# A new order for the first batch's steps and transfers in an attention and dense kernel on one core

## The chip, the cores and the metric

The kernel runs on one core of a Trainium2 chip. The core has a matrix engine (PE, TensorE), three engines for the rest (DVE or VectorE, ACT or ScalarE, POOL or GpSimd) and an engine that issues transfers (SP). Each works through a queue of its own in the order in which the program was written. The metric is the device time of one execution in microseconds (us), the median of three runs.

## What is computed

```python
def _attn_ref(q, k, v):                      # each (8, 8, 576, 64)
    k_p = k.reshape(B, H, Sp, pool, D).mean(axis=3)     # pool = 8: 72 keys
    v_p = v.reshape(B, H, Sp, pool, D).mean(axis=3)
    scores = scale * np.matmul(q, k_p.transpose(0, 1, 3, 2))
    scores = scores - np.max(scores, axis=-1, keepdims=True)
    attn = np.exp(scores)
    attn = attn / (np.sum(attn, axis=-1, keepdims=True) + 1e-09)
    return np.matmul(attn, v_p)
...
    x = attn_out.transpose(0, 2, 1, 3).reshape(B * S, H * D)     # 4608 x 512
    h = x @ w_in                                                  # 512 x 2048
    g = h * (1.0 / (1.0 + np.exp(-1.702 * h)))
    return g @ w_out                                              # 2048 x 512
```

Each batch's attention gives 576 rows of `x`; the dense layer takes these rows in chunks of 512.

## The kernel before

The work is written as a list of small steps. A table, `ORDER` (from line 27), names all 4763 of them in one row: `V:nm0_0#2` is the third `nm` step of batch 0, piece 0, on DVE. The letters are A for ACT, V for DVE, G for POOL, P for PE, D for a transfer that SP issues and O for an output; a star gives the step to the other engine that can do it. `Plan.order` (line 555) takes the steps by name in this order, and each engine's queue is what is left of the list when only its own steps are read. A step that stands later on its engine never overtakes one that waits. A second table, `WARMS` (line 462), puts extra passes of PE in front of named steps (16 ahead of the first `tps`, of two passes each); they multiply a constant, `ident`, by itself into a tile that nobody reads then, `warm` (`keep_warm`, line 2115).

The first batch runs through these steps, whose names the text uses:

- `kv`, `tl`, `q`: transfers of keys and values, of the rows that are left over at the end of the 576, and of queries. `raw`: a part of the weights, 512 KB of 64-bit numbers, `raw0`, `raw1` and so on.
- `red`: sums over windows of eight keys. DVE does the first key tile (`red0_k0`, line 882), PE the others (line 892) by multiplying with `ident`. `kbd`, `vbd` (line 928), `tps` (PE, line 958) and `tbd` (line 967): the sums spread into blocks, and the same of the left-over rows.
- `kps`, `k` and `qps`, `qt`: transposes on PE, and their copies on ACT or DVE.
- `sps`: scores on PE (line 1136). `nm` (line 1159): the negative maximum; `sc` (1167): the subtraction; `exp` on ACT (1188); sums (1193), the inverse, and `main` and `tail` (1208), the weights of the softmax in two groups of keys, on DVE.
- `tpt`, `apt` (PE, 1280): transposes of these; `at`, `ah` (1310, 1358): their copies; `pav` (PE, 1383, 1386): the product with the values; `x` (1423 on ACT, 1426 on DVE): the operand of the dense layer in two parts.
- Decoding of a part of the weights: ACT `e` and `raw` (1611, 1618), DVE `e` and `raw` (1624, 1630), POOL `raw` (1637), a cast `w` (1644, ACT or DVE) and POOL's `w` (1651). 32 parts go through it in all.
- `h` (PE, 1685 to 1687): the first product of the dense layer, in three passes, and `o` (1727 to 1729): the second.

Of PE's accumulators a pool `ps_o` of four banks holds, under one name `o`, the tiles `tps`, `qps`, `sps`, `tpt` and `apt` of this batch, the warm passes' tile and the dense layer's `o` tiles. A second pool of two banks holds `red`, the decoder's `e` and `h`; a third one of two `kps` and `pav`. A tile takes a bank when the one before it in that bank has been read. The warm passes' tile is made when the first pass is emitted, which `WARMS` puts ahead of `tps`, and it later serves as the accumulator of one row block of `o`.

```python
    warm = buf(ps_o, [P, DM], F32, "o", "warm")

    def keep_warm():
        nc.tensor.matmul(warm()[:, 0:P], lhsT=ident, rhs=ident, start=True, stop=True)
```

Of the kernel before, what the change touches and what calls it, by code (L numbers as in the profile page):

```python
# [27 lines left out]
D:raw#0 V:members#0 D:kv0#1 D:kv0#0 D:kv0#3 V:red0_k0#0 P:warm#0 D:tl0#0 D:tl0#1 A:e#0 V:at0_1#0 V:kbd0#0 D:kv0#2  # L28
V:e#0 P:tps0#0 D:q0_0#1 D:raw#1 P:red0_k1#0 V:tbd0#0 V:at0_0#0 A:raw#0 D:q0_0#0 D:raw#2 V:raw#0 P:kps0_0#0 D:kv0#5
P:qps0_0#0 V:kbd0#1 A:e#1 P:qps0_0#1 A:raw#1 G:raw#0 V:e#1 *A:qt0_0#0 A:k0_0#0 P:kps0_1#0 V:raw#1 D:raw#4 P:sps0_0#0  # L30
A:qt0_0#1 P:sps0_0#1 V:nm0_0#0 A:w#0 A:k0_1#0 P:qps0_0#2 V:nm0_0#1 G:w#0 V:sc0_0#0 D:kv0#4 A:e#2 A:qt0_0#2 P:qps0_0#3
P:sps0_0#2 V:e#2 D:kv0#6 D:kv0#7 D:q0_2#0 A:raw#2 A:qt0_0#3 V:sc0_0#1 V:raw#2 D:q0_1#1 P:sps0_0#3 A:e#4 D:q0_1#0
D:raw#6 A:raw#4 D:raw#5 V:nm0_0#2 D:raw#3 G:raw#1 V:e#4 V:nm0_0#3 P:red0_v0#0 A:sc0_0#0 V:sc0_0#2 V:raw#4 G:raw#2
P:red0_v1#0 D:raw#8 V:sc0_0#3 P:qps0_1#1 P:qps0_1#0 V:vbd0#0 D:raw#7 A:sc0_0#1 V:sps0_0#0 A:w#1 A:w#2 V:sps0_0#1
D:raw#13 A:qt0_1#1 G:raw#4 V:sps0_0#2 A:qt0_1#0 V:main0_0#3 V:main0_0#2 D:raw#10 V:tail0_0#0 A:e#6 V:main0_0#1
V:main0_0#0 P:tpt0_0#0 A:at0_0#0 V:vbd0#1 G:w#2 *A:w#4 V:e#6 D:qr1_0#3 D:qr1_0#6 P:apt0_0#2 P:sps0_1#0 A:ah0_0#2
P:apt0_0#3 V:nm0_1#0 D:qr1_0#1 A:at0_1#0 *A:ah0_0#3 A:raw#6 D:raw#12 P:pav0_0#2 V:raw#6 A:e#5 V:e#5 G:w#4 P:pav0_0#3
P:apt0_0#0 D:qr1_0#2 A:raw#5 D:tl1#1 A:x0_0#2 P:qps0_1#2 V:sc0_1#0 D:raw#9 A:e#3 D:qr1_0#4 P:apt0_0#1 V:x0_0#2
D:raw#11 A:ah0_0#0 A:x0_0#3 V:raw#5 A:raw#3 V:e#3 P:pav0_0#0 A:ah0_0#1 G:raw#6 P:sps0_1#1 V:x0_0#3 D:raw#14 A:e#8
G:w#1 D:raw#20 P:pav0_0#1 P:qps0_1#3 A:qt0_1#2 D:qr1_0#0 A:x0_0#0 P:sps0_1#2 A:raw#8 V:raw#3 G:raw#5 V:e#8 A:e#7  # L40
A:x0_0#1 V:x0_0#0 A:raw#7 D:raw#17 V:raw#8 V:e#7 D:raw#16 V:x0_0#1 V:raw#7 G:raw#3 P:h0_0#0 V:nm0_1#1 D:raw#15
P:h0_0#1 P:h0_0#2 A:w#6 P:h0_0#3 D:raw#18 P:h0_0#4 A:w#3 P:h0_0#5 A:e#10 V:nm0_1#2 G:raw#8 V:sc0_1#1 V:e#10 A:qt0_1#3
A:raw#10 G:w#6 P:h0_0#6 G:w#3 P:h0_0#7 V:raw#10 V:sc0_1#2 P:sps0_1#3 A:w#8 P:h0_0#8 P:h0_0#9 A:sc0_1#0 P:h0_0#10
A:g0_0#0 D:raw#22 P:h0_0#11 V:nm0_1#3 V:sc0_1#3 D:qr1_0#7 P:h0_0#12 V:sps0_1#0 P:h0_0#13 *A:gh0_0#0 G:raw#7 G:w#8
G:raw#10 *G:gl0_0#0 D:raw#21 A:sc0_1#1 *A:w#10 P:h0_0#14 D:qr1_0#5 *A:w#5 D:kv1_0#1 G:w#10 P:h0_0#15 D:raws#2
V:sps0_1#1 P:h0_0#16 A:g0_0#1 V:sps0_1#2 V:main0_1#1 P:h0_0#17 A:gh0_0#1 G:w#5 P:h0_0#18 A:e#9 D:tl1#0 D:raws#1
A:raw#9 P:h0_0#19 V:tail0_1#0 A:w#7 P:o0_0#0 P:o0_0#1 V:main0_1#0 P:h0_0#20 V:main0_1#2 D:raw#19 P:h0_0#21 P:h0_0#22
P:tpt0_1#0 P:apt0_1#0 G:gl0_0#1 P:o0_128#0 P:o0_128#1 D:kv1_0#0 V:e#9 A:ah0_1#0 A:at0_1#1 V:raw#9 *A:at0_0#1 A:e#11
D:raw#26 P:apt0_1#1 A:ah0_1#1 G:w#7 A:raw#11 P:h0_0#23 A:g0_0#2 V:main0_1#3 P:pav0_1#0 V:e#11 A:x0_1#0 V:raw#11 A:e#12
P:o0_0#2 *A:left0_1#0 *A:gh0_0#2 G:raw#9 V:x0_1#0 A:w#9 V:e#12 G:gl0_0#2 P:pav0_1#1 P:o0_128#2 A:raw#12 P:apt0_1#2  # L50
P:o0_0#3 A:e#14 G:w#9 *A:x0_1#1 A:ah0_1#2 D:raw#23 P:o0_128#3 V:raw#12 V:x0_1#1 V:e#14 D:raw#25 P:apt0_1#3 A:e#13
A:raw#14 V:e#13 P:o0_0#4 V:raw#14 A:left0_1#1 A:ah0_1#3 G:raw#12 V:qt1_0#0 A:raw#13 V:raw#13 P:pav0_1#2 A:e#15
A:raw#15 P:pav0_1#3 P:h0_256#0 A:x0_1#2 A:x0_1#3 G:raw#11 V:e#15 V:raw#15 A:e#16 V:x0_1#2 D:qr1_0#11 G:raw#13
P:h0_256#1 A:raw#16 V:x0_1#3 G:raw#14 P:o0_128#4 P:h0_256#2 A:left0_1#2 P:h0_256#3 P:h0_256#4 V:e#16 P:h0_256#5 A:w#11
V:raw#16 *A:w#12 V:qt1_0#1 P:h0_256#6 P:tps1#0 P:h0_256#8 P:h0_256#7 G:raw#16 D:qr1_0#14 *G:w#11 A:g0_256#0 P:h0_256#9
P:h0_256#10 A:gh0_256#0 P:h0_256#11 V:tbd1#0 A:e#21 P:o0_128#5 V:red1_0#0 P:h0_256#12 D:kv1_1#1 V:e#21 A:w#13 V:kbd1#0
A:raw#21 V:raw#21 G:w#12 P:h0_256#13 D:qr1_0#10 P:h0_256#14 P:h0_256#15 D:qr1_0#9 G:gl0_256#0 P:o0_0#5 A:g0_256#1
*A:w#14 P:o0_256#0 P:warm0_256#0 G:raw#15 A:gh0_256#1 P:o0_256#1 D:qr1_0#13 G:w#14 D:qr1_0#8 A:vt1#0 *G:gl0_256#1
D:kv1_1#0 A:e#17 V:e#17 P:kps1_0#0 A:e#19 P:warm0_256#1 V:e#19 A:raw#17 A:k1_0#0 P:warm0_256#2 V:raw#17 P:sps1_0#0
A:raw#19 A:e#18 A:raw#18 V:raw#19 P:o0_256#2 V:e#18 V:raw#18 V:nm1_0#0 G:w#13 P:h0_0#24 A:w#16 P:h0_0#25 A:w#15  # L60
*A:left0_1#3 G:raw#21 G:raw#19 V:qt1_0#2 A:e#20 P:h0_0#26 G:w#15 D:qr1_0#15 P:h0_0#27 G:raw#17 V:sc1_0#0 P:h0_0#28
P:h0_0#29 P:h0_0#30 P:h0_0#31 A:raw#20 V:e#20 V:raw#20 P:o0_256#3 V:red1_1#0 V:kbd1#1 A:g0_0#3 A:gh0_0#3 G:gl0_0#3
G:w#16 A:e#23 A:raw#23 V:e#23 V:raw#23 P:sps1_0#1 V:nm1_0#1 V:sc1_0#1 G:raw#23 P:warm0_256#3 P:h0_256#16 P:h0_256#17
P:h0_256#18 D:qr1_0#12 P:h0_256#19 P:o0_128#6 A:e#22 V:e#22 A:raw#22 V:raw#22 P:kps1_1#0 A:k1_1#0 G:raw#18 P:h0_256#20
P:h0_256#21 P:h0_256#22 G:raw#22 P:h0_256#23 A:g0_256#2 A:gh0_256#2 G:gl0_256#2 P:o0_128#7 P:h0_256#24 P:h0_256#25
P:h0_256#26 P:h0_256#27 D:tl2_0#1 D:raw#27 V:qt1_0#3 D:raw#24 D:kv1_0#2 D:kv1_0#3 V:red1_0#1 P:o0_0#6 A:e#31 A:raws#1
V:e#31 A:w#18 D:tl2_0#2 V:raws#1 P:o0_0#7 G:w#18 A:e#24 A:w#17 V:vbd1#0 V:e#24 D:qr1_1#7 D:wd2_3#0 A:raw#24
P:h0_256#28 P:h0_256#29 V:vt1#0 P:h0_256#30 P:h0_256#31 A:g0_256#3 P:sps1_0#2 D:raws#0 D:qr1_1#0 D:wd1_0#0 P:sps1_0#3
V:raw#24 V:nm1_0#2 A:e#26 G:raw#20 A:w#20 G:w#20 *A:gh0_256#3 *G:w#17 P:warm0_256#4 P:warm0_256#5 G:gl0_256#3
P:o0_256#4 P:o0_256#5 P:h0_0#32 P:h0_0#33 V:e#26 A:raw#26 V:raw#26 P:h0_0#34 P:h0_0#35 G:raw#26 A:w#22 G:raw#24  # L70
*A:w#19 G:w#19 V:nm1_0#3 V:sc1_0#2 P:warm0_256#6 P:warm0_256#7 V:sc1_0#3 P:o0_256#6 A:e#27 A:raw#27 V:e#27 P:o0_256#7
D:tl2_0#3 V:raw#27 A:g0_0#4 A:gh0_0#4 G:gl0_0#4 P:h0_0#36 P:h0_0#37 P:h0_0#38 D:qr1_1#1 D:kv1_1#3 D:qr1_1#2 D:kv1_1#2
V:red1_1#1 D:qr1_1#3 V:qt1_1#0 D:0_1#0 D:qr1_1#6 P:sps1_1#0 D:qr1_1#5 D:qr1_1#4 V:qt1_1#1 D:tl2_0#0 P:h0_0#39 D:raw#28
A:sc1_0#0 V:sm1_0#0 V:sm1_0#1 V:main1_0#1 V:main1_0#0 V:vbd1#1 A:e#25 V:tail1_0#0 A:raw#25 V:e#25 V:raw#25 A:w#21
D:wd3_3#0 D:qr1_1#13 D:qr1_1#14 P:warm0_0#0 D:qr1_1#11 A:g0_0#5 A:gh0_0#5 G:gl0_0#5 P:o0_0#8 D:wd4_0#0 P:o0_256#8
P:tpt1_0#0 *G:w#22 V:nm1_1#0 V:sc1_1#0 G:w#21 A:e#30 V:e#30 D:kv2_0#0 D:raw#29 A:raws#0 V:raws#0 P:o0_128#8 D:qr1_1#8
A:at1_0#1 V:tred2_0#0 P:h0_0#40 A:at1_0#0 V:at1_0#1 V:at1_0#0 A:vh1#0 P:h0_0#41 A:w#24 G:w#24 G:raw#25 P:sps1_1#1
V:nm1_1#1 V:sc1_1#1 P:h0_0#42 P:h0_0#43 A:g0_0#6 A:gh0_0#6 G:gl0_0#6 P:o0_0#9 P:h0_0#44 A:e#28 V:e#28 A:w#26
D:qr1_1#15 D:qr1_1#12 D:kv2_0#1 V:qt1_1#3 G:vl1#0 A:raw#28 V:raw#28 A:w#23 G:w#23 A:e#29 V:e#29 A:raw#29 V:raw#29
P:apt1_0#2 P:h0_0#45 P:h0_0#46 P:h0_0#47 A:g0_0#7 P:apt1_0#1 A:ah1_0#1 P:o0_256#9 D:qr1_1#9 P:o0_128#9 P:warm0_0#1  # L80
P:warm0_0#2 P:o0_128#10 P:h0_0#48 P:h0_0#49 P:h0_0#50 P:h0_0#51 G:raw#27 G:raw#29 V:al1_0#1 A:ah1_0#2 V:al1_0#2
P:pav1_0#2 *G:w#26 D:qr1_1#10 V:qt1_1#2 A:w#25 *G:w#25 A:gh0_0#7 G:raws#1 A:e#32 P:o0_0#10 V:e#32 V:tbd2_0#0 A:raws#2
# [2548 lines left out]
```

## Time and profile before

| | us |
|---|---|
| median of 3 runs | 874.46 (873.82 to 874.91) |
| the profiled execution | 873.51 |
| its span, first to last instruction | 871.4 |
| PE busy, share of the span | 864.3 (99%) |
| DVE busy | 752.5 (86%) |
| ACT busy | 527.4 (61%) |
| POOL busy | 364.7 (42%) |

The share is an average over the whole span. The opening, in which the first batch's attention has to be done before there is anything for the dense layer, is less than 4% of it, so the shares hardly show it; it has to be read from stretches and timelines that start at zero. In those, a step's duration contains its tail: the start of one step to the start of the next on the same engine is what it takes of that engine's time when there is no gap.

### The profile page before, as it was taken

To read this page: it belongs to the slowest core of one execution; us is meant where nothing else is said; L and a number is where in the kernel's file an instruction comes from. 1 tells how busy PE (TensorE), PEld (TensorE's weight loads), DVE (VectorE), ACT (ScalarE), POOL (GpSimd) and SP (SyncE) were. 2 spreads that over 40 slices of the span, in tenths; PEclk is the share of its full clock that TensorE was granted. 3 is DMA by queue.
4 is the path that set the end of the run, shared out by engine and by line. 5 is a ranking of instruction groups with operands and counts; after the bars stand their busy time and mean duration, and the time that the engine had idled before them with its cause. 6 is when DMAs were issued, how large, how long until landed. Compare 5 with 4: busy or idle time off the path is not lost.

```text
span 871.4 us, 15966 instructions
## 1 busy us (share of the span) xinstructions
PE 864.3 (99%) x5466; PEld 779.6 (89%) x5466; DVE 752.5 (86%) x1432; ACT 527.4 (61%) x1159; POOL 364.7 (42%) x355
## 2 busy tenths in 40 slices
...
GB/s 278 363 242 201 161 40 193 205 142 201 235 217 188 218 179 215 260 162 221 193 263 194 191 246 269 274 276 294 258 294 219 267 307 287 294 25 25 102 141 49
DMA packets 150319, 182.71 MB, mean 210 GB/s; under 512 B 85600, under 2 KB 98912, under 8 KB 150240
## 3 DMA queue, kind: packets, MB, share of 16 engines
...
## 4 chain that ended last, share of the span: by engine, by line
PE 95%; DVE 3%; DMA 1%; issue 0%; SPq 0%; DVEq 0%
PE m L2462 14%; PE ha L1899 13%; PE hb L1899 10%; PE o L2156 7%; PE o L2157 7%; PE o L2158 7%; PE la L2230 5%; PE sps L1136 4%; PE h L1685 3%; PE h L1686 3%; PE h L1687 3%; PE o L1728 3%; PE o L1727 3%; PE o L1729 3%; PE lc L2230 3%; PE lb L2230 1%
## 5 line engine op out<-in xcount | busy, mean ns | idle before, releaser
L1962 POOL TENSOR_TENSOR glall<-shared,ghall 128x256 fp32r<-128x256 f32 x60 | 47.5, 797 | 175.0 <-ACT shared L1955 124.9
L2156 PE MATMUL o<-w,ghall 128*128 128x512 f32 x256 | 101.4, 396 | 0.0
L2157 PE MATMUL o<-w,ghall 128*128 128x512 f32 x256 | 100.9, 394 | 0.0
L2158 PE MATMUL o<-w,glall 128*128 128x512 f32 x256 | 99.9, 390 | 0.0
L1899 PE MATMUL ha<-xs,ws 128*128 128x256 f32 x480 | 71.5, 285 | 0.0
L1899 PEld LDWEIGHTS ha<-xs,ws 128*128 128x128 f32 x480 | 64.6, 190 | 4.4 <-ACT gs L1914 0.7
L1962 POOL TENSOR_TENSOR glall<-gall,ghall 128x256 fp32r<-128x256 f32 x26 | 21.6, 831 | 110.2 <-ACT gall L1955 93.7
L1899 PE MATMUL hb<-x,ws 128*128 128x256 f32 x480 | 67.0, 284 | 0.0
L1899 PEld LDWEIGHTS hb<-x,ws 128*128 128x128 f32 x480 | 62.4, 191 | 1.5 <-DVE gall L1921 0.3
L1715 POOL TENSOR_TENSOR gl<-g,gh 128x512 fp32r<-128x512 f32 x27 | 37.9, 1403 | 49.2 <-ACT gh L1707 40.3
L2158 PEld LDWEIGHTS o<-w,glall 128*128 128x128 f32 x256 | 48.1, 188 | 10.9
L1685 PE MATMUL h<-x,w 128*128 128x512 f32 (+1 forms) x160 | 57.2, 358 | 0.2 <-DVE raw L1630 0.2
L1687 PE MATMUL h<-x,w 128*128 128x512 f32 (+1 forms) x160 | 55.6, 347 | 0.0
L1686 PE MATMUL h<-x,w 128*128 128x512 f32 (+1 forms) x160 | 55.5, 347 | 0.0
L2156 PEld LDWEIGHTS o<-w,ghall 128*128 128x128 f32 x256 | 48.4, 189 | 5.5
L2157 PEld LDWEIGHTS o<-w,ghall 128*128 128x128 f32 x256 | 48.5, 189 | 5.1
L1251 ACT COPY main<-sc 32x256 f32<-32x256 f32 (+2 forms) x104 | 47.1, 453 | 4.5 <-DVE sc L1208 2.9
L1947 ACT ACTIVATE ghall<-shared 128x256 fp32r<-128x256 f32 x86 | 35.4, 415 | 18.3 <-DVE shared L1921 13.5
L1136 PE MATMUL sps<-k,qt 128*128 128x144 f32 x320 | 45.8, 287 | 0.1
L1727 PE MATMUL o<-w,gh 128*128 128x512 f32 x112 | 45.4, 405 | 0.0
L1136 PEld LDWEIGHTS sps<-k,qt 128*128 128x128 f32 x320 | 42.9, 190 | 2.5 <-issue 0.5
L1728 PE MATMUL o<-w,gh 128*128 128x512 f32 x112 | 43.8, 391 | 0.0
(277 smaller groups left out, 2609.0 us busy)
## 6 DMA issues: line engine op xcount, KB each, us to landing
ws<-wd SPq DMA_DIRECT2D x144, 512.0 KB
shared<-wd SPq DMA_DIRECT2D x48, 256.0 KB
wd<-stage SPq DMA_DIRECT2D x16, 512.0 KB
raw<-in_moe_w_in_dram SPq DMA_DIRECT2D x15, 512.0 KB
raw<-in_moe_w_out_dram SPq DMA_DIRECT2D x15, 512.0 KB
kv_False<-in_k_dram SPq DMA_DIRECT2D x28, 256.0 KB
kv_True<-in_v_dram SPq DMA_DIRECT2D x28, 256.0 KB
out_dram<-osb ACTq DMA_DIRECT2D x24, 256.0 KB
```

What stands on the lines that cost most here:

```text
L1136: nc.tensor.matmul(ps()[:, t * PW : (t + 1) * PW], lhsT=qt()[:, s0 : s0 + P], rhs=m.k2()[:, jj], start=True, stop=True,)
L1685: nc.tensor.matmul(o, lhsT=w[:, 0, j], rhs=xs[:, 0], start=j == 0, stop=False)
L1686: nc.tensor.matmul(o, lhsT=w[:, 1, j], rhs=xs[:, 0], start=False, stop=False)
L1687: nc.tensor.matmul(o, lhsT=w[:, 0, j], rhs=xs[:, 1], start=False, stop=j == NJ - 1)
L1727: nc.tensor.matmul(o, lhsT=gh()[:, i, tok], rhs=w[:, 0], start=f == 0, stop=False)
L1728: nc.tensor.matmul(o, lhsT=gh()[:, i, tok], rhs=w[:, 1], start=False, stop=False)
L1899: nc.tensor.matmul(o, lhsT=wv()[:, r, jj], rhs=xo(k, jj), start=start and n == 0, stop=n == len(terms) - 1,  skip_group_check=not start,)
L2156: nc.tensor.matmul(o(), lhsT=gh()[:, tok], rhs=w()[:, 0], start=start, stop=False)
L2157: nc.tensor.matmul(o(), lhsT=gh()[:, tok], rhs=w()[:, 1], start=False, stop=False)
L2158: nc.tensor.matmul(o(), lhsT=gl()[:, tok], rhs=w()[:, 0], start=False, stop=stop)
L2230: nc.tensor.matmul(bank(), lhsT=wv()[:, r, jj], rhs=xs[jj]()[:, k], start=start and n == 0, stop=n == len(terms) - 1, skip_group_check=not ...
L2462: nc.tensor.matmul(banks[i]()[:, i], lhsT=av(r)[:, i * P : (i + 1) * P], rhs=tv(k), start=p == 0 and n == 0 and (i == 0 or banks[0] is not ...
```

## The change

The first 560 steps of `ORDER` stand in another order; the 4203 behind them, from `P:h0_0#39`, stay word for word as they were. It is the same set of steps, and `WARMS` and all other code are the same. The star moves with it: some copies, casts and splits that ACT or POOL had are now DVE's and the other way about (`ah0_0#2` and `w#7` to DVE, `ah0_0#3` and `w#14` back, for example). The explicit step `P:warm#0`, which was PE's first one, now stands behind `h0_0#21`; the extra passes of `WARMS` stay ahead of `tps`.

```diff
@@ ORDER, the first 560 of 4763 steps @@
-D:raw#0 V:members#0 D:kv0#1 D:kv0#0 D:kv0#3 V:red0_k0#0 P:warm#0 D:tl0#0 D:tl0#1 A:e#0 V:at0_1#0 V:kbd0#0 D:kv0#2
-V:e#0 P:tps0#0 D:q0_0#1 D:raw#1 P:red0_k1#0 V:tbd0#0 V:at0_0#0 A:raw#0 D:q0_0#0 D:raw#2 V:raw#0 P:kps0_0#0 D:kv0#5
...
+D:kv0#3 V:members#0 D:tl0#0 V:at0_1#0 D:tl0#1 V:at0_0#0 P:tps0#0 V:tbd0#0 D:raw#0 A:e#0 A:raw#0 D:kv0#2 V:e#0 V:raw#0
+G:raw#0 A:w#0 D:kv0#0 D:kv0#1 D:q0_0#0 V:red0_k0#0 V:kbd0#0 P:red0_k1#0 D:q0_0#1 P:qps0_0#0 *A:qt0_0#0 V:kbd0#1
...
```

The transfers now come in the order: a key tile (`kv0#3`), both `tl`, `raw0`, three key tiles, both `q`, `raw1`, `raw2`, `raw4`, then values, the second piece of `q`, values, and weights. Before it was `raw0`, three `kv`, both `tl`, `kv`, `q`, `raw1`, `q`, `raw2` and then values.

DVE, opening, before. `kv0` to `red0_k0` is the sum of the first key tile, `e0` and `raw0` belong to the first part of the weights:

```order
L882 TENSOR_TENSOR kv0_161<-kv0_161 128x2x256
L882 TENSOR_TENSOR kv0_161<-kv0_161 128x2x128
L882 TENSOR_TENSOR red0_k0_168<-kv0_161 128x128
L1266 MEMSET at0_1_177 128x320
L928 TENSOR_TENSOR kbd0_179<-red0_k0_168,mask2i_84 128x256
L1624 TENSOR_SCALAR e0_175<-e0_175 128x512
L967 TENSOR_TENSOR tbd0_214<-tps0_199,mask_90 128x512
L1266 MEMSET at0_0_216 128x320
L1630 SCALAR_TENSOR_TENSOR raw0_155<-raw0_155,e0_175 128x512
L928 TENSOR_TENSOR kbd0_179<-red0_k1_205,mask2i_84 128x256
```

The same place after:

```order
L1266 MEMSET at0_1_163 128x320
L1266 MEMSET at0_0_166 128x320
L967 TENSOR_TENSOR tbd0_187<-tps0_185,mask_90 128x512
L1624 TENSOR_SCALAR e0_191<-e0_191 128x512
L1630 SCALAR_TENSOR_TENSOR raw0_189<-raw0_189,e0_191 128x512
L882 TENSOR_TENSOR kv0_200<-kv0_200 128x2x256
L882 TENSOR_TENSOR kv0_200<-kv0_200 128x2x128
L882 TENSOR_TENSOR red0_k0_207<-kv0_200 128x128
L928 TENSOR_TENSOR kbd0_209<-red0_k0_207,mask2i_84 128x256
L1115 COPY qt0_0_0_226<-qps0_0_0_223 128x256
L928 TENSOR_TENSOR kbd0_209<-red0_k1_211,mask2i_84 128x256
```

`tbd`, `e0` and `raw0` went ahead of the sum; two copies `qt` stand where one part of the weights (`e1`) stood.

DVE, where the softmax begins, before. `nm` and `sc` are the maximum and the subtraction of the score tiles `sps`:

```order
L1624 TENSOR_SCALAR e1_236<-e1_236 128x512
L1115 COPY qt0_0_0_244<-qps0_0_0_232 128x256
L1630 SCALAR_TENSOR_TENSOR raw1_203<-raw1_203,e1_236 128x512
L1159 TENSOR_REDUCE nm0_0_264<-sps0_0_0_256 128x2x2
L1159 TENSOR_REDUCE nm0_0_264<-sps0_0_1_261 128x2x2
L1167 TENSOR_TENSOR sc0_0_274<-sps0_0_0_256,nm0_0_264 128x2x144
L1624 TENSOR_SCALAR e2_277<-e2_277 128x512
L1167 TENSOR_TENSOR sc0_0_274<-sps0_0_1_261,nm0_0_264 128x2x144
L1630 SCALAR_TENSOR_TENSOR raw2_220<-raw2_220,e2_277 128x512
L1159 TENSOR_REDUCE nm0_0_264<-sps0_0_2_287 128x2x2
```

The same place after, from the first `nm`:

```order
L1159 TENSOR_REDUCE nm0_0_249<-sps0_0_0_246 128x2x2
L1624 TENSOR_SCALAR e1_251<-e1_251 128x512
L1167 TENSOR_TENSOR sc0_0_256<-sps0_0_0_246,nm0_0_249 128x2x144
L1630 SCALAR_TENSOR_TENSOR raw1_239<-raw1_239,e1_251 128x512
L1159 TENSOR_REDUCE nm0_0_249<-sps0_0_1_269 128x2x2
L1624 TENSOR_SCALAR e2_279<-e2_279 128x512
L1159 TENSOR_REDUCE nm0_0_249<-sps0_0_2_283 128x2x2
L1167 TENSOR_TENSOR sc0_0_256<-sps0_0_1_269,nm0_0_249 128x2x144
L1167 TENSOR_TENSOR sc0_0_256<-sps0_0_2_283,nm0_0_249 128x2x144
L1159 TENSOR_REDUCE nm0_0_249<-sps0_0_3_294 128x2x2
```

`e1` and `raw1` stand behind the first `nm` and not ahead of it, and so does one `e2` between the others; `e4` went out of this place.

PE, from the first transpose of the softmax's weights, before:

```order
L1280 MATMUL apt0_0_2_401<-ident_79,main0_0_375 128x128 x2
L1136 MATMUL sps0_1_0_404<-k20_246,qt0_1_0_373 128x144 x3
L1280 MATMUL apt0_0_3_410<-ident_79,main0_0_375 128x128 x2
L1383 MATMUL pav0_0_2_422<-ah0_0_2_408,vbd0_355 128x256
L1386 MATMUL pav0_0_2_422<-at0_1_177,tbd0_214 128x256
L1383 MATMUL pav0_0_3_430<-ah0_0_3_417,vbd0_355 128x256
L1386 MATMUL pav0_0_3_430<-at0_1_177,tbd0_214 128x256
L1280 MATMUL apt0_0_0_433<-ident_79,main0_0_375 128x128 x2
L1108 MATMUL qps0_1_2_442<-ident_79,q0_1_301 128x128 x2
L1108 MATMUL qps0_1_2_442<-ident_79,q0_2_294 128x64
L1280 MATMUL apt0_0_1_453<-ident_79,main0_0_375 128x128 x2
```

The same place after:

```order
L1280 MATMUL apt0_0_2_384<-ident_79,main0_0_350 128x128 x2
L1280 MATMUL apt0_0_3_392<-ident_79,main0_0_350 128x128 x2
L1136 MATMUL sps0_1_0_405<-k20_244,qt0_1_0_340 128x144 x3
L1280 MATMUL apt0_0_0_415<-ident_79,main0_0_350 128x128 x2
L1383 MATMUL pav0_0_3_421<-ah0_0_3_395,vbd0_315 128x256
L1386 MATMUL pav0_0_3_421<-at0_1_163,tbd0_187 128x256
L1280 MATMUL apt0_0_1_429<-ident_79,main0_0_350 128x128 x2
L1108 MATMUL qps0_1_2_432<-ident_79,q0_1_323 128x128 x2
L1108 MATMUL qps0_1_2_432<-ident_79,q0_2_326 128x64
L1383 MATMUL pav0_0_2_436<-ah0_0_2_387,vbd0_315 128x256
L1386 MATMUL pav0_0_2_436<-at0_1_163,tbd0_187 128x256
```

Two `apt`, `sps0_1_0` and a third `apt` now come in one run, and the first `pav` behind them; before, two `pav` stood between the second and the third `apt`.

## Rows read from the trace of the kernel before

**Rows 1.** The table of stretches: us, then each engine's busy us (instructions), clock, DMA.

```profile
14.29:23.43 9.14, 8.90 (x69) 7.83 (x68) 8.89 (x21) 6.78 (x14) 5.53 (x5) 1.00 1.00 308
23.43:32.16 8.73, 8.43 (x50) 6.66 (x50) 8.68 (x19) 8.21 (x20) 5.86 (x6) 1.00 1.07 372
32.16:54.79 22.63, 22.30 (x139) 18.98 (x138) 21.63 (x43) 22.07 (x38) 18.29 (x16) 1.00 1.07 359
...
100.00:160.00 60.00, 59.87 (x305) 50.45 (x305) 51.50 (x95) 34.11 (x65) 35.82 (x34) 1.00 0.42 130
```

**Rows 2.** PE's waits up to 160 us: total, times, longest.

```profile
PE tps L958 <- DMA tl<-in_k_dram: 1.5, 1, 1.5
...
PE h L1685 <- DVE raw L1630: 0.2, 1, 0.2
```

**Rows 3.** Timeline of the opening: start, duration, engine, line, operation, tiles, [idle before].

```profile
1.35 5.77 PE L2116 MATMUL warm<-ident 128*128 128x128 f32 x34 [1.35 <-POOL ident masks.py:199]
...
6.55 1.15 DVE L882 TENSOR_TENSOR kv<-kv 128x512 f32<-128x512 f32 x2 [3.52 <-DMA kv<-in_k_dram]
...
8.33 0.36 DVE L928 TENSOR_TENSOR kbd<-red_k,mask2i 128x256 f32<-128x256 f32 x1
...
8.66 1.10 PE L958 MATMUL tps<-tl,members 128*128 128x512 f32 x2 [1.54 <-DMA tl<-in_k_dram]
...
9.60 1.95 PE L892 MATMUL red_k<-kv,ident 128*128 128x128 f32 x16
...
9.80 0.69 DVE L967 TENSOR_TENSOR tbd<-tps,mask 128x512 f32<-128x512 f32 x1 [0.51 <-PE tps L958]
```

**Rows 4.** Timeline of DVE through the softmax to the first operand.

```profile
14.29 0.95 DVE L1159 TENSOR_REDUCE nm<-sps 128x4 f32<-128x288 f32 x2 [0.36 <-PE sps L1136]
...
15.52 0.69 DVE L1624 TENSOR_SCALAR e<-e 128x512 uint32<-128x512 uint32 x1
16.11 0.45 DVE L1167 TENSOR_TENSOR sc<-sps,nm 128x288 f32<-128x288 f32 x1
16.48 0.68 DVE L1630 SCALAR_TENSOR_TENSOR raw<-raw,e 128x512 uint32<-128x512 uint32 x1
17.07 0.45 DVE L1159 TENSOR_REDUCE nm<-sps 128x4 f32<-128x288 f32 x1
...
23.10 0.74 DVE L1208 TENSOR_TENSOR main<-sc,sps 128x256 f32<-128x256 f32 x2
...
30.80 0.41 DVE L1426 TENSOR_TENSOR x<-pav,x 128x256 fp32r<-128x256 f32 x1
```

**Rows 5.** The table of stretches for the warm passes at the start.

```profile
1.35:4.93 3.58, 3.58 (x16) 3.58 (x17) 1.60 (x7) 0.91 (x2) 0.00 (x0) 1.00 0.86 249
4.93:7.12 2.19, 2.19 (x19) 2.00 (x18) 0.57 (x1) 0.98 (x2) 0.00 (x0) 1.00 1.01 297
```

**Rows 6.** DMA issues of the first 15 us: transfers and their size.

```profile
raw<-in_moe_w_in_dram SPq DMA_DIRECT2D x3, 512.0 KB
kv<-in_k_dram SPq DMA_DIRECT2D x4, 256.0 KB
...
tl<-in_v_dram SPq DMA_DIRECT2D x1, 128.0 KB
```

**Rows 7.** Timeline of PE behind the softmax.

```profile
24.00 0.41 PE L1280 MATMUL apt<-ident,main 128*128 128x128 f32 x2 [0.28 <-DVE main L1208]
...
24.98 0.38 PE L1280 MATMUL apt<-ident,main 128*128 128x128 f32 x2
...
32.16 0.38 PE L1685 MATMUL h<-x,w 128*128 128x256 f32 x1
```

**Rows 8.** Timeline of ACT behind the softmax.

```profile
24.44 0.37 ACT L1358 COPY ah<-apt 128x256 f32<-128x256 f32 x1 [0.33 <-PE apt L1280]
...
25.23 0.68 ACT L1618 ACTIVATE raw<-raw 128x512 uint32<-128x512 uint32 x1
25.81 0.62 ACT L1611 ACTIVATE e<-raw 128x512 f32<-128x512 f32 x1
```

150 lines of the change are left out of this document (75 added, 75 removed).

## The prediction

> **What bounds the kernel now.** I read the table of stretches first, then PE's waits, then the timelines of single engines up to the first product of the dense layer. From 32.16 us, where the first `h` product starts [rows 7], PE (TensorE) is all but full: it idles 0.33 us up to 54.79 us, and 0.13 us between 100 and 160 us [rows 1]. So whatever the first batch does ahead of 32.16 us reaches the end almost one to one: the order is worth what it does to the start of the first `h`, plus what PE loses later. Ahead of it the limit changes hands. Until 8.66 us PE waits for a transfer: 1.5 us, for `tl` [rows 2, 3]. From `nm` at 14.29 us to the softmax's `main` DVE (VectorE) has no gap: 8.89 of 9.14 us, then 8.68 of 8.73 us, while ACT (ScalarE) is at 6.78 and then 8.21 us [rows 1]. DVE's steps there start one right behind another, 0.60 us for an `e` or a `raw`, some 0.36 us for `nm` and `sc` [rows 4]. So between 14.3 and 32.2 us the number of DVE steps that stand in line ahead of the first `h` is the price of the order, and PE, the engine that is full afterwards, follows DVE and ACT here.
>
> **The change part by part.** The steps are the same; only their order is new, so each term is a shift.
>
> (a) Transfers and start. Transfers move at 297 GB/s around 6 us and 308 later [rows 1, 5], call it 0.3 MB per us. Before, a `raw` and three `kv` went ahead of both `tl`, 1.25 MB by the sizes in [rows 6]; now one `kv`: 1 MB less, about 3.3 us earlier. Then it is the warm passes that hold `tps`: 34 passes take 1.35 to 7.1 us [rows 3]; now 32 stand ahead of it, so `tps` starts near 6.8 instead of 8.66 us, 1.9 us earlier. The whole tile of `q` no longer has `raw1` ahead of its second half: 0.5 MB less, about 1.6 us earlier. The price is the key tile that DVE sums itself (`red0_k0`): another two `kv` and both `tl` now go ahead of its end, 0.75 MB or 2.5 us, so it starts not at 6.55 us [rows 3] but at 9.1 at the earliest.
>
> (b) DVE's opening. Now `tbd`, `e0` and `raw0` stand ahead of that sum. With `tps` done near 7.8 us, `tbd` starts at 7.8, `e0` at 8.5 (0.69 us of `tbd` [rows 3]), `raw0` at 9.25, when ACT and the later landing of `raw0` allow it, and the sum starts at about 9.85 us. Before, from the start of the sum to the start of `kbd` it was 8.33 - 6.55 = 1.78 us and 0.36 us for `kbd` [rows 3]: now `kbd` ends near 11.9 us. Before, `kbd` was done long before PE had summed the second key tile, 16 passes from 9.60 us [rows 3], and `kps` followed these. That sum on PE now waits as well, since its bank is the one that `e0` lies in until `raw0` has read it, a pause on PE from 7.8 to about 10.0 us. `kps` then lies near 12.5, the copy of `k` and the first `sps` behind it near 13.9, and `nm` starts at 14.6 instead of 14.29: **+0.3 us**. The 1.9 us won by `tps` and the 1.6 us by `q` end in this wait.
>
> (c) The softmax chain. Before, `e1` and `raw1` ran on DVE ahead of the first `nm`, and it still idled 0.36 us for PE there [rows 4]. Now they stand between `nm`, `sc` and `nm`. That is 0.60 us each (from 15.52 to 16.11 and from 16.48 to 17.07 in [rows 4]), on a queue without gaps. The second of the sums and the order of `main` and `tail` give back about 0.2. Last `main`: 23.43 before (the second of the pair at 23.10 in [rows 4]), about 24.7 now: **+1.0 us** beyond (b). The transposes `apt`, which waited for it at 24.00 [rows 7], start at 25.3.
>
> (d) From `apt` to `h`. Before, 24.00 to 32.16 is 8.16 us with PE at 8.43 of 8.73 us in about that stretch [rows 1, 7]: PE hardly waited. The ring `o` has four banks, but the program takes one of them for the warm passes ahead of `tps`, both before and after, and keeps it; three are left for `tpt`, `apt`, `qps` and `sps`. The trace shows three: the second `apt` starts at 24.98, when `ah` on ACT (24.44, 0.37 us) has emptied the bank [rows 7, 8]. Now the order takes `apt`, `apt`, `sps`, `apt` in one run (shown in the section on the change) and so needs its fourth bank one step earlier: `sps0_1#0` waits for ACT's `ah0_0#3` at 26.5 us, the third `apt` for DVE's `ah` behind `e6`, at 27.2, the fourth for `at` on ACT at 28.3, `qps0_1#2` for `ah0_0#0` at 30.1, which now stands on ACT behind `e5`, `raw5`, `e3`, `x` and `raw3` (0.58 us from a `raw` to the next step, [rows 8]); then the four `pav`, and the last of them, `pav0_0#1`, needs the bank of `x0_0#2`. Walking all three queues with the trace's steps gives the first `h` at 35.9 us, 3.7 us late, of which 2.4 belong to this part.
>
> The walk is an upper bound, since each wait is added at its full size. A lower one is DVE's line alone: before, the first `h` operand's `x` starts at 30.80 us, 16.5 us behind `nm` [rows 4]. After, two `e` and two `raw` more stand between them (`e1`, `raw1`, `raw8`, `e7`): 14.6 + 16.5 + 4 x 0.60 = 33.5, `h` behind it at 33.9, 1.7 us late. I take 35.4, nearer to the walk, because it is built of waits that the program does have: **+3.2 us for (b) to (d)**.
>
> (e) Afterwards. The two extra pairs are then done, and all decoded weights have more time. PE can get back what it idles up to 160 us: 0.33 + 0.13 = **-0.5 us** [rows 1]. One warm pass pair moves from the start into the full stretch, two starts of 0.11 us (19 starts in 2.19 us, [rows 5]): **+0.2 us**. What the new places of later transfers cost (`tl` and `wd` among others) I put at nothing: up to 160 us PE's list of waits has one for a transfer, that for `tl`, and behind 32 us only one of 0.2 us [rows 2].
>
> Sum on the profiled execution: 873.5 + 3.2 - 0.5 + 0.2 = 876.4 us. The median of the three runs lies 0.95 us above it (874.46 against 873.51), so 877.4 us.
>
> **Rivals.** *Absorbed:* DVE's line alone decides, the bank waits of (d) are hidden behind it. For it: DVE is the one engine without a gap; against it: the order of the `o` banks. 873.5 + 1.7 - 0.5 + 0.2 + 0.95 = 875.9 us; less if `e1` and `raw1` find a gap, 874.7.
>
> *Faster, the other side:* the earlier `tl` and `q` are carried through. `tps` starts 1.9 us earlier and if all steps kept that lead, the end would be 874.46 - 1.9 = 872.5 us. It decides if the first `nm` starts at 12.4 instead of 14.6. For it: the longest wait of PE is this one [rows 2]. Against it: `red0_k0` cannot start before its own transfer near 9.1, and its 2.1 us, a transpose, a copy and a score lie behind it.
>
> *The clock.* In the first 3.58 us PE starts 16 warm passes, then 19 in 2.19 us: half the rate and the full one, though the granted clock reads 1.00 in both, the 2.4 GHz level [rows 5]. The pause of 1.54 us ahead of `tps` did not bring the low rate back: 16 passes of `red_k` take 1.95 us [rows 3]. The new pause is about 2.2 us. If it does, the next 16 passes lose 16 x (0.224 - 0.115) = 1.7 us: 879.1 us. The Trainium skill ("TensorE: Matmul & The Clock Gate", section "HAM oscillation — how this bites in real kernels") says that a wait for data that is long enough lets the clock drop, so that the next group of matmuls starts at the low rate. By that rule the new pause is a risk that the old one was not; no row here shows a pause of that length, so I give it one in ten.
>
> *The change does not do what it says* (the start gains nothing, because the warm passes or DVE's memsets hold `tps`): then `tps` stays near 8.7, `tbd` and all behind it come 1.9 us later, and the time is about 879 us; its small chance goes with the clock's.
>
> **How the numbers follow.** Forecast, `h` late by 2.5 us or more: 0.54, 877.4 us. Absorbed: 0.27, 874.7 to 875.9. Faster: 0.09, 872.5. Clock or no earlier start: 0.10, 879. A measurement tells 0.2%, 1.75 us, from no change: the band is 872.7 to 876.2. Slower gets the forecast and the last case, 0.64; same gets absorbed, 0.27; faster 0.09. The range reaches from 873.7, under absorbed, to 879.7, over the walk's full 3.7 us (877.9) and the clock's 1.7 us: it leaves out the faster case and the worst sums.
>
> **What would show it.** In the changed profile: `tps` near 6.8 us; PE idle from about 7.8 to 10.0; the sum L882 at about 9.9; first `nm` at 14.6; last `main` at 24.7; several PE waits for ACT and DVE between 26 and 33 us; first `h` near 35.4; PE full behind it. It would be wrong if `nm` comes at 13 us or earlier, if the stretch from `apt` to `h` stays near 8.2 us, if PE loses more than 1 us between 36 and 160 us, or if its passes behind the pause run at the low rate.

## The result and the profile after

| | before | after |
|---|---|---|
| median | 874.68 us (6 runs) | 881.06 us (879.42 to 881.40, 6 runs) |
| ratio | | 1.0066 (1.0049 to 1.0083) |
| profiled execution | 873.51 us | 881.37 us |
| first `tps` / first `nm` / first `apt` | 8.66 / 14.29 / 24.00 us | 6.66 / 14.73 / 25.21 us |
| first `h` | 32.16 us | 37.42 us |
| DVE busy | 752.5 us | 756.3 us |

The kernel is 5.8 us slower by the ratio; the forecast was 3 us, and the time lies above its range. The sign came as forecast, and in this execution the first half of the path; the loss is nearly twice as large.

Columns in what follows are those of the rows ahead of the prediction. First the table of stretches of the changed kernel:

```profile
26.00:37.00 11.00, 9.02 (x40) 6.88 (x41) 8.84 (x17) 7.94 (x19) 6.18 (x6) 0.84 1.05 387
37.00:60.00 23.00, 23.00 (x147) 20.03 (x146) 21.80 (x45) 21.43 (x35) 18.38 (x16) 1.00 1.01 315
60.00:105.00 45.00, 44.83 (x267) 38.66 (x266) 42.76 (x68) 33.00 (x57) 34.13 (x29) 1.00 0.60 172
105.00:165.00 60.00, 59.02 (x300) 49.82 (x301) 52.90 (x97) 32.78 (x64) 35.25 (x33) 1.00 0.41 132
```

Against [rows 1], the stretch ahead of the first `h` (26 to 37 us) now has PE busy 9.02 of 11 us, DVE 8.84 and ACT 7.94: nobody is full any more, so these engines wait for each other. The granted clock there is 0.84. From 37 to 105 us PE is as full as before; from 105 to 165 us it idles 0.98 us where it idled 0.13 between 100 and 160 [rows 1]. PE's waits of the first 170 us say who holds it:

```profile
PE red_k L892 <- DVE raw L1630: 2.4, 1, 2.4
PE qps L1108 <- ACT ah L1358: 1.7, 1, 1.7
...
PE sps L1136 <- DVE sc L1167: 1.1, 1, 1.1
PE apt L1280 <- DVE main L1208: 0.5, 1, 0.5
PE sps L1136 <- ACT ah L1358: 0.5, 1, 0.5
```

In place of the 1.5 us for a transfer [rows 2] there are two long waits for DVE (2.4 and 1.1 us) and two for ACT; `apt` waited for `main` before as well, 0.28 us [rows 7]. The opening, to be held against [rows 3]:

```profile
6.66 1.02 PE L958 MATMUL tps<-tl,members 128*128 128x512 f32 x2
...
8.56 0.70 DVE L1624 TENSOR_SCALAR e<-e 128x512 uint32<-128x512 uint32 x1
...
9.91 1.87 DVE L882 TENSOR_TENSOR kv<-kv 128x512 f32<-128x512 f32 x2
...
10.04 2.05 PE L892 MATMUL red_k<-kv,ident 128*128 128x128 f32 x16 [2.36 <-DVE raw L1630]
10.13 1.37 POOL L1637 TENSOR_TENSOR raw<-raw 128x512 uint32<-128x512 uint32 x1 [8.82 <-DVE raw L1630]
```

`tps` starts 2.0 us earlier, the sum of the first key tile (L882) 3.4 us later, and PE's sum of the second stands for 2.36 us until DVE's `raw0` is done. One thing is not as in the rows of before: the first two steps of the tree take 1.87 us instead of 1.15, all of it in the second (1.14 us instead of 0.42), and POOL's `raw` runs beside them. DVE in the softmax, against [rows 4]:

```profile
14.73 0.46 DVE L1159 TENSOR_REDUCE nm<-sps 128x4 f32<-128x288 f32 x1 [0.58 <-PE sps L1136]
15.10 0.69 DVE L1624 TENSOR_SCALAR e<-e 128x512 uint32<-128x512 uint32 x1
15.70 0.45 DVE L1167 TENSOR_TENSOR sc<-sps,nm 128x288 f32<-128x288 f32 x1
16.06 0.68 DVE L1630 SCALAR_TENSOR_TENSOR raw<-raw,e 128x512 uint32<-128x512 uint32 x1
...
23.99 1.07 DVE L1208 TENSOR_TENSOR main<-sc,sps 128x256 f32<-128x256 f32 x3
```

`e1` and `raw1` stand in the chain at 0.60 us each (15.10 to 15.70, 16.06 to 16.66), and the last of the three `main` starts near 24.7 us. PE behind it, against [rows 7]:

```profile
25.21 0.63 PE L1280 MATMUL apt<-ident,main 128*128 128x128 f32 x4 [0.54 <-DVE main L1208]
26.30 1.00 PE L1136 MATMUL sps<-k,qt 128*128 128x144 f32 x6 [0.46 <-ACT ah L1358]
...
28.41 0.38 PE L1280 MATMUL apt<-ident,main 128*128 128x128 f32 x2
30.47 0.64 PE L1108 MATMUL qps<-ident,q 128*128 128x128 f32 x3 [1.68 <-ACT ah L1358]
...
31.58 0.59 PE L1386 MATMUL pav<-at,tbd 128*128 128x256 f32 x2
...
32.78 1.06 PE L1386 MATMUL pav<-at,tbd 128*128 128x256 f32 x2
...
37.42 0.37 PE L1685 MATMUL h<-x,w 128*128 128x256 f32 x1
```

`sps`, and then `qps`, wait for an `ah` of ACT, 0.46 and 1.68 us. The `pav` pair at 32.78 lasts 1.06 us, where 0.59 is usual (as at 31.58): this is where the granted clock was low. Last, a place that the prediction did not look at closely, the neighbourhood of 103 us:

```profile
102.83 1.30 POOL L1715 TENSOR_TENSOR gl<-g,gh 128x512 fp32r<-128x512 f32 x1 [4.56 <-ACT gh L1707]
103.03 1.65 DVE L1651 TENSOR_TENSOR w<-raw,w 128x512 fp32r<-128x512 f32 x1
...
105.97 0.97 PE L1136 MATMUL sps<-k,qt 128*128 128x144 f32 x6 [1.15 <-DVE sc L1167]
```

DVE's `w` (part 22 of the weights) takes 1.65 us, started 0.2 us behind a POOL step; PE's `sps` needs the `sc` that stands behind it on DVE, and waits 1.15 us. In the kernel before DVE has the same step, but starts it 0.12 us ahead of POOL's:

```profile
98.21 0.69 DVE L1651 TENSOR_TENSOR w<-raw,w 128x512 fp32r<-128x512 f32 x1
98.33 1.73 POOL L1715 TENSOR_TENSOR gl<-g,gh 128x512 fp32r<-128x512 f32 x1 [5.29 <-ACT gh L1707]
```

### The profile page after: what moved, and what is told of

Read it like the earlier page. It is cut to its first block, busy times and chain, and to the rows that moved or that the text cites. A ratio compares the mean times of both kernels' runs of the same rounds, so it can differ in the third digit from the quotient of the medians.

```text
span 879.3 us, 15969 instructions
## 1 busy us (share of the span) xinstructions
PE 866.5 (99%) x5466; PEld 779.9 (89%) x5466; DVE 756.3 (86%) x1437; ACT 524.9 (60%) x1152; POOL 368.5 (42%) x357
## 4 chain that ended last, share of the span: by engine, by line
PE 89%; DVE 4%; DMA 2%; SPq 2%; issue 1%; ACT 1%; DVEq 0%; ACTq 0%
PE m L2462 13%; PE ha L1899 12%; PE hb L1899 9%; PE o L2156 6%; PE o L2157 6%; PE o L2158 6%; PE la L2230 5%; PE sps L1136 4%; PE h L1685 3%; PE h L1686 3%; PE h L1687 3%; PE o L1729 3%; PE o L1727 3%; PE o L1728 3%; PE lc L2230 2%; PE lb L2230 1%
## 5 line engine op out<-in xcount | busy, mean ns | idle before, releaser
L1727 PE MATMUL o<-w,gh 128*128 128x512 f32 x112 | 45.1, 402 | 0.0
L1729 PE MATMUL o<-w,gl 128*128 128x512 f32 x112 | 43.9, 392 | 0.0
```

What stands on the lines that cost most here:

```text
L1727: nc.tensor.matmul(o, lhsT=gh()[:, i, tok], rhs=w[:, 0], start=f == 0, stop=False)
L1729: nc.tensor.matmul(o, lhsT=gl()[:, i, tok], rhs=w[:, 0], start=False, stop=f == NF - 1)
```

## The experiments

All times are ratios to the kernel before, run beside it; 0.1% is 0.87 us.

| run | what it is | ratio (95%) | over before |
|---|---|---|---|
| the change | | 1.0066 (1.0049 to 1.0083) | 5.8 us |
| early_new | new up to `tpt` | 1.0020 (1.0011 to 1.0030) | 1.7 |
| late_new | new from `tpt` | 1.0053 (1.0036 to 1.0070) | 4.6 |
| toh_new | new up to `h` | 1.0053 (1.0038 to 1.0068) | 4.6 |
| fromh | new from `h` | 1.0022 (1.0010 to 1.0033) | 1.9 |
| fill | passes in a late pause | 1.0070 (1.0055 to 1.0085) | 6.1 |
| open_fill | passes in the early pause | 1.0062 (1.0049 to 1.0076) | 5.4 |
| chain_e1 | before, `e1` and `raw1` behind `nm` | 1.0011 (1.0002 to 1.0021) | 1.0 |
| few_warm | fewer idle passes | 1.0069 (1.0051 to 1.0087) | 6.0 |
| bank_free | the same, bank not held | 1.0039 (1.0023 to 1.0055) | 3.4 |
| w22_pool | the step at 103 us given to POOL | 1.0037 (1.0024 to 1.0051) | 3.2 |
| both_fixed | both of these | 1.0020 (1.0010 to 1.0030) | 1.7 |
| late_fixed | the same behind the old opening | 1.0009 (1.0001 to 1.0018) | 0.8 |

**Which part of the order costs what.** Four kernels join the two orders: one order up to a step, and behind it all other steps in the sequence of the other.

```diff
 ... V:main0_0#2 V:main0_0#3 P:red0_v1#0 P:tpt0_0#0
-V:main0_0#0 A:qt0_1#1 D:raw#6 G:raw#4 *A:w#4 G:w#4
+P:warm#0 D:raw#6 D:raw#5 D:raw#3 D:raw#8 D:raw#7 D:raw#13 A:qt0_1#1
```

This is the joint of early_new, against the changed kernel.

> The new order up to the first transpose of the softmax's weights (tpt0_0#0), the old one behind it. If the late start of h has its parts as the prediction had them (1.3 us from the opening and the softmax chain, the rest from the order of the banks behind it), the first apt starts near 25.2 us as in the changed kernel, the first h near 33.5, PE shows no wait over 0.5 us between 26 and 33 us, its granted clock stays at 1.00 there, and the time is 1 to 1.5 us over the kernel before (875.8). If the opening alone is what hurts, h starts at 36 or later and the time is near 880.

Measured: 1.7 us over before (1.0 to 2.6), a little above what was expected; PE has no wait over 0.5 us there. PE's rows, 1 us later than expected because `nm` starts at 15.74 us in this execution:

```profile
26.22 0.41 PE L1280 MATMUL apt<-ident,main 128*128 128x128 f32 x2 [0.39 <-DVE main L1208]
...
34.38 0.37 PE L1685 MATMUL h<-x,w 128*128 128x256 f32 x1
```

The old sequence behind `tpt` takes 8.16 us from the first `apt` to the first `h`, as it did before (24.00 to 32.16), whatever the time at which it starts. So the waits of the changed kernel there are not an echo of its late softmax: the old order does not have them behind the same late start.

> The old order up to tpt0_0#0, the new one behind it. Bank order: apt at 24.0, then PE waits for ACT and DVE between 25 and 31 us as in the changed kernel, h 2.4 us late or 3.9 with a fall of the clock, 34.5 to 36, and the time 877.5 to 879.5. If the waits only came from the later softmax, h starts near 32.2 to 33 and the time is within 1 us of before.

```diff
 ... A:e#6 V:main0_0#1 V:main0_0#0 P:tpt0_0#0
-A:at0_0#0 V:vbd0#1 G:w#2 *A:w#4 V:e#6 D:qr1_0#3
+G:w#2 *A:w#4 G:w#4 V:vbd0#1 V:e#6 P:apt0_0#2 *A:ah0_0#2
```

This diff is against the kernel before. Measured: 4.6 us over it, with the same waits on the list (1.2 us of `qps` for `ah`, 0.5 of `sps` for `ah`, 1.2 of `sps` for DVE's `sc`). With early_new that makes 6.3 us for the two halves, against 5.8 for the whole: they add up within the intervals.

The second pair has its joint at the first `h`.

> The new order up to the first h, the old one behind it, so that only the steps ahead of the first product of the dense layer are new. h at 37.4 as in the changed kernel. If the new places and the additional DVE steps behind h cost something of their own, the time is 1 to 2.5 us below the changed kernel (878.5 to 880); if everything is lost ahead of h and the rest is its echo, it equals the changed kernel's (881).

```diff
 ... V:raw#7 P:sps0_1#2 V:nm0_1#2 P:h0_0#0
-P:h0_0#1 P:h0_0#2 V:nm0_1#1 A:qt0_1#3 A:w#6 P:sps0_1#3
+P:warm#0 D:raw#13 D:qr1_0#3 D:qr1_0#6 D:qr1_0#1 D:raw#12
```

Measured: 4.6 us, 1.2 less than the changed kernel, a difference that the two intervals alone do not tell from none. In its profile `h` starts at 38.05 us.

> The old order up to the first h, the new one behind it: the counterpart of toh_new. h at 32.2 as before. If the places behind h cost something by themselves, PE has one wait of about 1.1 us for sc on DVE near 99 us and the time is 1.1 to 1.5 us over before; if they cost only in company of a late h, the time is within 0.5 us of before.

```diff
 ... V:x0_0#1 V:raw#7 G:raw#3 P:h0_0#0
-V:nm0_1#1 D:raw#15 P:h0_0#1 P:h0_0#2 A:w#6 P:h0_0#3
+G:raw#8 V:nm0_1#2 P:h0_0#1 P:h0_0#2 V:nm0_1#1 A:qt0_1#3
```

Measured: 1.9 us over before. The order behind `h` costs something by itself. (In the profiled execution, 880.04 us where the median is 877.14, `h` starts at 35.88 us and not at 32.2: `qps` waits 1.7 us for `q` near 14 us. The opening differs between executions of one order: the first `nm` starts between 14.29 and 17.91 us in the profiles of before, late_new, late_fixed and fromh, which share the old opening. So a start of `h` in a single profile is worth less than the timed median.) The two profiles show where. In fromh (old up to `h`), around 102 us:

```profile
101.96 1.29 POOL L1715 TENSOR_TENSOR gl<-g,gh 128x512 fp32r<-128x512 f32 x1 [4.55 <-ACT gh L1707]
102.16 1.64 DVE L1651 TENSOR_TENSOR w<-raw,w 128x512 fp32r<-128x512 f32 x1
...
105.11 0.97 PE L1136 MATMUL sps<-k,qt 128*128 128x144 f32 x6 [1.15 <-DVE sc L1167]
```

and the same steps in toh_new (new up to `h`):

```profile
103.67 0.68 DVE L1651 TENSOR_TENSOR w<-raw,w 128x512 fp32r<-128x512 f32 x1
...
103.78 1.73 POOL L1715 TENSOR_TENSOR gl<-g,gh 128x512 fp32r<-128x512 f32 x1 [4.89 <-ACT gh L1707]
```

Where DVE's `w` starts 0.11 us ahead of POOL's `gl`, it takes 0.68 us and POOL's step 1.73, as in the kernel before; where it starts 0.2 us behind, it takes 1.64 and POOL's 1.29. Nine other profiles fall on the same two sides: with the old order behind `h` (before, early_new, chain_e1) PE has no such wait; with the new one and the step on DVE (the change, late_new, fill, open_fill, few_warm, bank_free) it has one of 1.15 to 1.22 us for `sc`. Whoever starts second is longer, by 0.43 us on POOL and by 0.96 on DVE. The Trainium skill ("SBUF — State Buffer", section "SBUF: two separate sides") says that a POOL step that reads SBUF and a DVE step with two SBUF inputs share a pair of ports, that the first one to start holds it for its whole instruction, and that the other one stands still until then. The trace agrees: POOL's step ends at 103.25 us in fromh, and DVE's, started at 102.16, ends 0.55 us behind that, at 103.80. What in the new order behind `h` moves the two steps by these 0.3 us against each other is not shown.

**The step at 103 us.** One star taken off, so that POOL does this `w`. The star stands in the kernel before too, so POOL gets a step here that it has in neither of the two kernels:

```diff
-P:tpt1_0#0 *G:w#22 V:nm1_1#0 V:sc1_1#0
+P:tpt1_0#0 G:w#22 V:nm1_1#0 V:sc1_1#0
```

> The changed kernel with one step, the last cast part of w22 (at 103 us, 1.65 us there against 0.69 before), back on POOL instead of DVE. PE's wait of 1.15 us at 105 us for sc on DVE stands behind that step: without it PE goes on, the lag against before stays at 4.6 us at 106 us, and the time falls by about 1.1 us, to 880. If the wait comes from DVE's load in general, or is made up for later, the time stays at 881.

Measured: 3.2 us over before, 2.6 less than the change. PE's busy time in the stretch from 98 to 108 us, the number behind the stretch's length, was 8.85 of 10 us in the changed kernel (first row) and is now whole (second):

```profile
98.00:108.00 10.00, 8.85 (x45) 6.91 (x45) 9.79 (x16) 7.59 (x14) 4.45 (x4) 1.00 0.70 201
98.00:108.00 10.00, 10.00 (x50) 8.00 (x49) 9.70 (x19) 8.66 (x16) 6.16 (x6) 1.00 0.65 189
```

The wait is gone, and the gain is not made up for later. It is larger than the 1.15 us of the wait, though the two intervals leave room for that; what the rest is, is not shown. The kernel before with this star off was not run; its PE idles only 0.13 us between 100 and 160 us [rows 1].

**The bank of the idle passes.** A pair of kernels. In both, the nine passes behind `tps` are gone; in the second, the 16 ahead of it write into the tile of `tps`, which is overwritten right afterwards, so that the tile `warm` takes its bank only at its own step, behind `h0_0#21`.

```diff
-WARMS = {"PE tps0#0": 16, "PE qps0_0#0": 2, "PE qps0_0#3": 3, "PE sps0_0#3": 1, "PE red0_v1#0": 1, "PE tpt0_0#0": 2}
+WARMS = {"PE tps0#0": 16}
...
-                keep_warm()
+                tps = next(b for b in t.bufs if b.name == "tps0")
+                nc.tensor.matmul(tps()[:, 0:P], lhsT=ident, rhs=ident, start=True, stop=True)
```

few_warm has the first two lines alone.

> The changed kernel without the idle PE passes behind the first tps (nine of them gone), the 16 ahead of tps kept in the tile of their own. It is the control for bank_free. Bank order and clock: the same waits for ACT and DVE between 26 and 33 us as in the changed kernel; the clock may fall more often, since PE has fewer passes in its pauses. h between 35.5 and 38, time 879 to 883.

> As few_warm, but the 16 passes ahead of tps write into the tile of tps itself, so that no bank of the ring o is held by them and the ring has four banks until h. Banks: sps0_1#0 starts right behind the second apt without its wait of 0.5 us, the wait of qps0_1#2 for ah0_0#0 (1.7 us) is gone or under 0.5, the first h is 1.5 to 2.6 us earlier than in few_warm, and the time with it. If the waits are those of ACT's and DVE's queues whatever the banks, h and the time equal few_warm's within 0.5 us.

Measured: 6.0 and 3.4 us over before, 2.6 us between them. PE in few_warm:

```profile
27.96 1.68 PE L1136 MATMUL sps<-k,qt 128*128 128x144 f32 x6 [0.46 <-ACT ah L1358]
...
33.01 0.64 PE L1108 MATMUL qps<-ident,q 128*128 128x128 f32 x3 [1.06 <-ACT ah L1358]
...
38.98 0.37 PE L1685 MATMUL h<-x,w 128*128 128x256 f32 x1
```

and in bank_free:

```profile
26.43 0.90 PE L1136 MATMUL sps<-k,qt 128*128 128x144 f32 x6
...
28.76 0.58 PE L1108 MATMUL qps<-ident,q 128*128 128x128 f32 x3
...
34.72 0.37 PE L1685 MATMUL h<-x,w 128*128 128x256 f32 x1
```

The two waits for `ah` are gone and `h` starts 4.3 us earlier in these two executions. Some of that is the clock, which fell in the profile of few_warm and not in the other, so the timed 2.6 us is the number to keep. The time from the first `apt` to the first `h` leaves the opening out and agrees better between profiles. It is 8.16 to 8.18 us with the old order there (before, early_new, chain_e1, fromh), 10.60 to 10.63 with the new one where the granted clock stayed at 1.00 (late_new, toh_new, open_fill, w22_pool), 12.1 to 12.2 where it fell (the change, few_warm), and 8.75 and 8.96 with the bank free (bank_free, both_fixed; 10.00 in late_fixed, with a wait told of below). So the new order costs 2.4 us there, and the held bank is 1.6 to 1.9 of them. The kernel before with its bank free was not run; its PE idles 0.30 us in that stretch [rows 1] and has little to gain.

**The softmax chain.** The kernel before with only two steps moved:

```diff
-V:e#1 *A:qt0_0#0 A:k0_0#0 P:kps0_1#0 V:raw#1 D:raw#4 P:sps0_0#0
+*A:qt0_0#0 A:k0_0#0 P:kps0_1#0 D:raw#4 P:sps0_0#0
...
-V:nm0_0#0 A:w#0 A:k0_1#0 P:qps0_0#2 V:nm0_0#1 G:w#0 V:sc0_0#0
+V:nm0_0#0 V:e#1 A:w#0 A:k0_1#0 P:qps0_0#2 V:nm0_0#1 G:w#0 V:sc0_0#0 V:raw#1
```

> The kernel before with e1 and raw1 of DVE moved behind the first nm, as the new order has them; all else stays. Chain: two steps of 0.60 us come into DVE's full queue, less what it idles ahead of nm: the last main starts 0.8 to 1.0 us later than at 23.4, apt and h as well, and the time rises by 0.8 to 1.0 us. If DVE has slack in the chain after all, the time stays within 0.3 us.

Measured: 1.0 us over before (1.0002 to 1.0021). The rows of this execution lie 1.8 us behind those of [rows 7], more than the timed difference, because `nm` starts 0.75 us later here; from there to the first `apt` it takes 10.77 us instead of 9.71, 1.06 more. Its first `apt` to first `h` is again 8.17 us:

```profile
25.81 0.41 PE L1280 MATMUL apt<-ident,main 128*128 128x128 f32 x2 [0.28 <-DVE main L1208]
...
33.98 0.38 PE L1685 MATMUL h<-x,w 128*128 128x256 f32 x1
```

**The clock.** Two kernels fill a pause of PE with idle passes, which go ahead of the waiting step and so need not delay it.

```diff
-WARMS = {"PE tps0#0": 16, "PE qps0_0#0": 2, "PE qps0_0#3": 3, "PE sps0_0#3": 1, "PE red0_v1#0": 1, "PE tpt0_0#0": 2}
+WARMS = {"PE tps0#0": 16, "PE qps0_0#0": 2, "PE qps0_0#3": 3, "PE sps0_0#3": 1, "PE red0_v1#0": 1, "PE tpt0_0#0": 2, "PE qps0_1#2": 7}
```

> The changed kernel with seven more idle passes of PE (14 matmuls of 0.11 us) in front of qps0_1#2, where it waits 1.7 us for ACT. Clock: with the pause filled, PE keeps the full rate through the pav products, the granted clock between 32 and 37 us is 1.00 instead of 0.68, the first h starts near 36.0 instead of 37.4, and the time falls by about 1.4 us. If the low rate there has another cause, or DVE and ACT hold h anyway, h stays at 37.4 and the time at 881.

Measured: 6.1 us over before, no gain. The stretches of its profile (the granted clock is the third number from the end):

```profile
10.00:15.00 5.00, 5.00 (x32) 4.93 (x31) 3.04 (x7) 0.93 (x2) 2.59 (x2) 0.66 1.05 333
24.00:28.00 4.00, 3.52 (x17) 3.55 (x18) 2.66 (x8) 2.21 (x5) 2.90 (x3) 0.59 0.99 368
32.00:38.00 6.00, 5.55 (x36) 4.66 (x35) 4.03 (x9) 4.14 (x12) 3.36 (x4) 1.00 1.06 401
```

The filled pause did its work, 1.00 from 32 to 38 us, but the clock had fallen twice ahead of it, behind the pause of the opening and behind a wait of 1.5 us for a `v` tile. And at the full rate a `pav` waits 0.4 us for an `ah` instead. open_fill puts nine passes, of two matmuls each, ahead of `red0_k1`:

```diff
-WARMS = {"PE tps0#0": 16, "PE qps0_0#0": 2,
+WARMS = {"PE tps0#0": 16, "PE red0_k1#0": 9, "PE qps0_0#0": 2,
```

> The changed kernel with 18 more idle matmuls of PE ahead of red0_k1, in the pause from 7.7 to 10.0 us. Clock: the pause is what lets the rate fall in some executions (0.66 to 0.68 of full between 10 and 15 us in two profiles of toh_new and fill, 1.00 in that of the changed kernel): with it filled, the granted clock there is 1.00, and the time is 0 to 1 us under the changed kernel's 881. If the passes themselves delay red0_k1, it starts behind 10.1 us and the time goes up by as much.

```profile
10.00:15.00 5.00, 3.54 (x30) 3.30 (x31) 4.32 (x7) 0.68 (x1) 2.41 (x2) 1.00 0.92 282
32.00:38.00 6.00, 5.55 (x33) 4.66 (x33) 4.38 (x10) 4.86 (x12) 3.46 (x4) 1.00 1.06 398
```

Full rate in both stretches of its profile, and 5.4 us over before: 0.4 us less than the change, which the intervals do not tell apart; `kps` now waits 1.2 us for DVE's `kbd`. The clock falls in some of these executions (1.00 between 10 and 15 us in the changed kernel's profile, the first row below, 0.68 in that of toh_new, the second, behind nearly the same pause), but it is not where the 5.8 us went. Of the six timed executions of the changed kernel the three with a mean granted clock of 1.000 took 879.53, 880.84 and 881.40 us, the three with 0.998 and 0.999 took 879.42, 881.28 and 881.37; and open_fill took 882.10 us in its profiled execution, at 1.000.

```profile
10.00:15.00 5.00, 4.93 (x42) 4.58 (x42) 3.92 (x8) 1.87 (x5) 2.67 (x2) 1.00 1.08 328
10.00:15.00 5.00, 4.30 (x25) 4.31 (x26) 3.33 (x6) 0.66 (x1) 2.65 (x2) 0.68 0.95 290
```

**Both causes taken away.** The edits of bank_free and w22_pool together, once on the changed kernel, once behind the old order up to `tpt0_0#0`.

> bank_free with w22's cast part back on POOL as well: both causes behind the opening taken away. If they are two costs that add up (2.6 us for the bank, 1.1 to 2.5 for the step at 103 us), what is left is the opening and the softmax chain, 1 to 1.8 us over before: first h near 34.5, no PE wait for sc at 103 us, the time 1.0 to 1.8 us over the kernel before. If DVE's load decides anyhow, the time stays 3 us over before.

Measured: 1.7 us over before. That it is early_new's number to the tenth is luck, with intervals of 0.9 us to either side. The first `h` starts at 35.26 us in the profile, 0.8 later than expected, and the wait for `sc` is gone. From few_warm's 6.0 us the two edits took 4.3.

> The old order up to tpt0_0#0 and the new one behind it, with the bank free and w22 on POOL. Causes as found: late_new's 4.4 us over before lose 2.6 and 1.1 to 2.5, so the time is -0.5 to +0.7 us from before, first h within 0.7 us of 32.2. If it is under before by more than 0.2%, the new order behind the softmax is better than the old one once its bank is there; if it is still 2 us over, another cost sits in the late part.

Measured: 0.8 us over before (1.0001 to 1.0018), just above what was expected. With its bank and its port conflict out of the way, the new order behind the softmax is about as good as the old one, not better. Its `h`, expected within 0.7 us of 32.2, starts at 34.70 in the profile: `q` came 1.1 us late there, and a `pav` waits 1.3 us for an `at` of ACT, a wait that no other profile has. No kernel tried here beats the kernel before.

## Why the prediction was wrong where it was

**Start, (a) and (b): the mechanism right, the agreement in part luck.** `tps` at 6.66 us (6.8 forecast), the pause on PE to 10.04 us (10.0), the sum at 9.91 (9.85), the first `nm` at 14.73 (14.6): the early `tl` and `q` end in the wait for `raw0` and for the key tile. But of the nine profiles with the new opening this one has the earliest `nm`; the others have it between 15.18 and 16.93 us. Timed, early_new's 1.7 us less chain_e1's 1.0 leave 0.7 for the opening, where 0.3 was forecast, with intervals that leave room for both. The tree's stretch from 1.15 to 1.87 us beside POOL's `raw` was not foreseen, since its price came from a place where POOL was idle; it cost little here, because PE's queue had `qps` ahead of `kps` anyway.

**The chain, (c): right.** 1.0 us forecast, 1.0 us timed in chain_e1, the last `main` near 24.7 us as forecast. Parts (b) and (c) together were 1.3 us; early_new times them at 1.7.

**The banks, (d): the mechanism right, its size cut by 0.5 us.** The walk put `sps0_1#0` at 26.5 us (26.30 in the trace), the third `apt` at 27.2 (27.14), the fourth at 28.3 (28.41) and `qps0_1#2` at 30.1 (30.47). It gave 10.6 us from the first `apt` to the first `h`, and the four profiles at the full clock have 10.60 to 10.63. Then the forecast took 35.4 us for `h` instead of 35.9, leaning towards the bound from DVE's line alone. The rows speak against that bound: between 26 and 37 us DVE itself waits in the changed kernel, busy 8.84 of 11 us. Without the fall of the clock, in the profile of w22_pool, `h` starts at 36.29 us; with it, at 37.42. bank_free times the held bank alone at 2.6 us. One reading under (d) does not hold: the `apt` at 24.98 us, cited for a ring of three banks, follows on `sps` without a wait, so that row does not show it; bank_free does.

**Afterwards, (e): this step failed.** It gave 0.5 us back, put the new places of later transfers at nothing because PE showed no wait there, and gave the new places of DVE's and POOL's steps no term at all. Of the 0.5 us, the 0.3 of the first stretch did come back: PE is full from 37 to 60 us. But the order behind `h` costs 1.2 us (the change against toh_new) to 1.9 (fromh) or 2.6 (w22_pool). What the runs show of it is the step at 103 us: DVE's `w`, started behind POOL's `gl` instead of ahead of it, takes 1.65 us instead of 0.69, and PE waits 1.15 us for the `sc` behind it. That alone is over the 1 us lost between 36 and 160 us which the prediction had named as a sign of being wrong. PE's lack of waits was read as slack, but a step of DVE that grew by 0.96 us reached PE whole: DVE was busy 42.84 of 45.21 us up to that place, in a row of the kernel before that the prediction did not use:

```profile
54.79:100.00 45.21, 45.21 (x271) 39.56 (x269) 42.84 (x70) 34.27 (x61) 32.01 (x27) 1.00 0.63 184
```

More load on DVE is not what the rows show: it is busy 42.76 us from 60 to 105 us in the changed kernel and 42.63 from 55 to 100 before.

**The rivals.** "Absorbed" falls with bank_free and late_new, "faster" with the opening. The clock did fall, in the changed kernel's profile behind the waits for `ah`, and elsewhere behind the opening's pause, so its mechanism is there, and there it makes `h` 1.5 to 1.6 us later in single executions; but filling either pause gained nothing that could be timed, and the executions at the full clock are no faster: it is no term of the median.

The sum as the runs have it: 1.7 us for opening and chain; 1.5 (both_fixed against w22_pool) to 2.6 us (bank_free against few_warm) for the bank; 1.2 to 2.6 us for the order behind `h`. The ends together make 4.4 to 6.9 us, with 5.8 measured. Against the forecast's terms, (b) and (c) were 0.4 us too small, (d) 0.5, and (e), at -0.3 us, 1.5 to 2.9: the largest part of what was missed.

What stays open: in several profiles, the changed kernel's among them, PE waits again for DVE near 620 and 640 us (1.15 and 0.46 us in the changed kernel), where that of before has nothing. The order there is the same in both. A late `h` alone does not bring these waits, since late_new (35.84 us) has none there; whether they come and go between executions was not tried. And neither the free bank nor the step on POOL was tried in the kernel before.
